# A fused attention and gated-MLP kernel: from the second batch on, product tiles of two banks, and three PSUM banks that gates and side work share in turn

## The chip, the cores and the metric

One core of one Trainium2 chip runs the kernel. The metric is device time in microseconds (us), the median of several runs. A difference of 0.3% (about 2.1 us) is about what a measurement of this kernel can tell from no change.

## What is computed

`x` has 4 batches of 12416 tokens with 128 channels; 32 inducing vectors attend to the tokens of a batch, and then the tokens attend to the 32 results. What comes out goes through a gated MLP with 1536 hidden columns.

```
def mab(q, kv):
    s = scale * (q @ kv.transpose(0, 2, 1))
    s = s - s.max(-1, keepdims=True)
    a = np.exp(s)
    a /= a.sum(-1, keepdims=True) + 1e-09
    return a @ kv
h = mab(I, x)                  # stage 1: 32 results for each batch
attn = mab(x, h)               # stage 2: each token attends to them
gate = 1.0 / (1.0 + np.exp(-(attn @ w_gate)))
val = attn @ w_val
out = (gate * val) @ w_out
```

## The kernel before

**The MLP is the main stream.** The tokens are cut into 97 blocks of 512 (24 in each batch, and one last block of the 4 x 128 tokens left over). The 1536 hidden columns are 12 tiles of 128. The product of h with the weights (`hwt`) is formed once per batch, so that gates and values come from the 32 attention weights of a token (`a2r`) directly: one matmul with 32 rows gives one tile of 128 hidden columns by 512 tokens, which is one PSUM bank. For each tile there are four pieces of work:

- TensorE fills the gate (`g_ps`) and the value (`v_ps`), L1022 in `hidden_mm`.
- ScalarE takes the tanh of half the gate into `t` (L1053; L1045 for a gate tile that stands alone).
- VectorE makes `u = (t + 1) * v` with one SCALAR_TENSOR_TENSOR (L1071, in `product`).
- TensorE multiplies `u` with the output weights and adds up in `acc_ps` (L1106, in `project`, four matmuls for a tile). After 12 tiles ScalarE copies the block out of PSUM (`o`, L1124) and SyncE sends it off.

**Steps.** A step is one value tile, one `u`, and so one VectorE instruction. Until step 608 (`T0`) steps are narrow: a tile of two banks (1024 wide) and a tile of one bank (512 wide) alternate, gates as well as values, so that a block has 8 steps. The eight PSUM banks are then `g2` and `v2` with two banks each, and `g1`, `v1`, `acc` and `m` with one. From `T0` on, in the last 21 blocks, steps are wide: a block has 6 steps of 1024; values alternate between `v2` and `vw` (two banks each), gates are single tiles in `gw0`, `gw1` and `gw2`, and `acc` keeps its bank. The bank `m` is gone by then.

**Side work.** While the MLP of one batch runs, stage 1 of the next batch and stage 2 of the groups to come are worked off beside it: a group is 16 times 128 tokens, four blocks. All of this passes through the bank `m`: scores of stage 2 (`s_ps`, L602, copied out by ScalarE at L636), scores of stage 1 (L236, with a maximum on VectorE, L248, and an exponential, L261, or a plain copy, L358), sums (`hp_ps`, L296, copied at L311 and L421), and small ones for the batch's end (L483, L561, L575). Other parts of it use no PSUM: the exponentials L662 and L407, a maximum on VectorE from SBUF (L389), and the work of GpSimd. The places are numbers: `at(slot, make, late)` puts a piece beside slot `slot`, which is two narrow steps, and `beside` calls it there. A block is four slots. Each engine works its instructions off in the order in which they are written (`manual_schedule`), and waits in place for what an instruction needs.

**Order in a step.** `product(t)` writes the two value matmuls, the gate fills of a later step and the `u`; then come tanh, `project` for the step before, and the side work. In the wide part a step `t` fills and takes the tanh of the single gates 2k+3 and 2k+4 (k is `t - T0`), while its own `u` uses gates 2k and 2k+1. A value tile can be filled once the `u` two steps back is done.

Of the kernel before, what the change touches and what calls it, by code (L numbers as in the profile page):

```python
# [16 lines left out]
P = 128  # L18
# [8 lines left out]
def kernel(  # L27
# [37 lines left out]
    class Banks:  # L65
        pools = {}

# [143 lines left out]
    plan = {}  # L211

    def at(slot, make, late=False):
        plan.setdefault((slot, late), []).append(make)
# [90 lines left out]
    def s1_sum_keep(b, s, hp):  # L305
        ng, w, R = s1_dims(s)
        width = C + 1 if b else C
        summed[b] += 1
        if b == 0 and at_col[s] >= EARLY:
            return hp[:, 0:C]  # L310
        nc.scalar.copy(out=hsts[b % 2][0:R, s1_place(b, s), 0:width], in_=hp[0:R, 0:width])  # L311

    def plan_stage1(b, s, score, total):
        st = {}
        full = groups[s][1] == GC

        def begin():
            st["s1"] = s1_score(b, s, "m")

        def weigh():  # L320
            st["a1T"] = s1_exp(b, s, st["s1"])

        def turn():
            if full:
                st["a1"] = s1_turn_dma(b, s, st["a1T"])
            else:
                st["a1"] = s1_turn_copy(s, s1_turn_pe(b, s, st["a1T"]))

        at(score, begin)
        soon = full  # L330
        at(score + (0 if soon else 1), weigh, late=full)
        at(score + (1 if soon else 2), turn)
        first, second, keep = total

        def part(k0, k1):
            if k0 == 0:
                st["hp"] = ps.tile([P, C + 1], F32, tag="m", name="hp_ps")
            s1_sum_pe(b, s, st["a1"], st["hp"], k0, k1)

        at(first, lambda: part(0, 2))  # L340
        at(second, lambda: part(2, 4))
        at(keep, lambda: s1_sum_keep(b, s, st["hp"]))


    def plan_shared(b, o, takes, tops, least, weighs, sums, holds, one, with_one):
# [11 lines left out]
        def keep(i):  # L357
            nc.scalar.copy(out=place(i), in_=st["s1"][:])  # L358

        def score_one():  # L360
            s1 = s1_score_pe(b, NG, "m")
            st["one"] = s1p.tile([P, 512], F16, tag="a1T", name="one").bitcast(F32)[0:m, 0:P]
            nc.scalar.copy(out=st["one"], in_=s1[0:m, 0:P])
# [55 lines left out]
        def hold(k):  # L419
            summed[b] += 1  # L420
            nc.scalar.copy(out=hst[:, no + k, :], in_=st["hp"][:])  # L421

        for i in range(len(SHARED[b])):
            at(o + takes[i], lambda i=i: score(i))
            at(o + takes[i], lambda i=i: keep(i), late=True)
            at(o + weighs[i], lambda i=i: weigh(i), late=True)
# [4 lines left out]
        at(o + one[1], weigh_one)  # L431
# [6 lines left out]
        for k, slot in enumerate(holds):  # L438
            at(o + slot, lambda k=k: hold(k))
# [68 lines left out]
    def plan_combine(b, lead, weights, joined, taken, fill):  # L508
# [42 lines left out]
        def weight():  # L551
            l_ps = ps.tile([P, 1], F32, tag="m", name="l_ps")
            nc.tensor.matmul(
                l_ps[:],
# [4 lines left out]
            )  # L559
            lx, near, off = (bp.tile([P, 1], F32, tag=f"l{k}", name=f"l{k}") for k in range(3))  # L560
            nc.scalar.copy(out=lx[:], in_=l_ps[:])  # L561
# [11 lines left out]
        def h_keep():  # L573
            hT16[b] = bp.tile([P, m], F16, tag="hT", name="hT")
            nc.scalar.copy(out=hT16[b][:], in_=st["h_ps"][:])  # L575

# [3 lines left out]
        def keep(hf):  # L580
            if hf == 0:
                st["hwt"] = bp.tile([P, NI, P], F16, tag="hw", bufs=B, name="hwt")
            hw_take(st["hwt"], hf, st["hw_ps"])
            if hf == 1:
# [3 lines left out]
        at(weights, weigh)  # L588
        at(joined, join)
        at(joined + 7, weight)  # L590
        at(taken, h_sum)
        at(taken, h_keep)
        for hf, (first, second) in enumerate(fill):
            at(first, lambda hf=hf: part(hf))
            at(second, lambda hf=hf: keep(hf), late=True)
# [115 lines left out]
    def plan_stage2(b, c, score, take, weigh, far=None, soon=False, lag=None, low=None):  # L711
# [30 lines left out]
        def keep():  # L742
            if far is None:
                room()
            s2_take(st["sc"], 0, GC, st["s2"])

# [17 lines left out]

        if far is not None:
            at(far, one)
            at(far + 1, lambda: s2_take(st["sc"], GC, NLO, st["s2"]))
        at(score, lambda: half(0, False))
        at(score + 1, lambda: half(GC // 2, not soon))
# [6 lines left out]
        at(weigh, exp, late=True)  # L776
# [258 lines left out]
    def ring_t(i, n):  # L1035
        c = i % 24 * BC
        return xn[B - 2][:, c : c + n * BC, :].rearrange("p (j a) c -> p j (a c)", a=BC)

    def single_fill(i):
        if i < len(singles):  # L1040
            hidden_mm(singles[i], "g")

    def single_gate(i):
        if i < len(singles):
            nc.scalar.activation(out=ring_t(i, 1), in_=singles[i]["g"][:], func=AF.Tanh, scale=0.5)  # L1045

    def gate(t):
        if t < T0 + 2:
            st = gates[t]
            st["t"] = ring_t(2 * (t - T0), st["cnt"]) if t >= T0 else tp.tile([P, st["cnt"], 512], F16, tag=f"t{st['cnt']}", name="t16")  # L1050
# [6 lines left out]
    def product(t):  # L1057
# [6 lines left out]
        else:  # L1064
            single_fill(2 * (t - T0) + 3)
            single_fill(2 * (t - T0) + 4)
            st["t"] = ring_t(2 * (t - T0), 2)
# [171 lines left out]
    assert not plan  # L1239
# [31 lines left out]
```

## Time and profile before

| | |
|---|---|
| median of 3 runs | 713.9 us (713.79 to 715.37) |
| span of the profiled execution | 712.4 us |
| VectorE (DVE) busy | 694.2 us, 97% |
| ScalarE (ACT) busy | 678.6 us, 95% |
| TensorE (PE) busy, matmuls | 649.5 us, 91% |
| GpSimd (POOL) busy | 449.2 us, 63% |
| first `u` starts | 30.4 us |
| step 192 (second batch) starts | about 201 us |
| step 608 (`T0`) starts | 564.7 us |

The profiled execution's own time is not listed beside its profile; its span from the first to the last instruction is 1.5 us under the median of the runs. An instruction's duration in these views runs from its start until its result is out, and on ScalarE and VectorE the next one can start before that: the distance from one start to the next is what an instruction costs its engine, and it is shorter than its duration. "Busy" is the time in which at least one instruction is under way.

### The profile page before, as it was taken

Reading aid. Unit: us, or ns where it says so; the run is one execution under the profiler, and the core shown is the slowest. Engines: PE = TensorE matmul, PEld = TensorE weight load, DVE = VectorE, ACT = ScalarE, POOL = GpSimd, SP = SyncE. Lnnn points to the kernel's source line nnn. Section 1 sums busy time; section 2 is a strip of 40 time slices with the busy share of each in tenths; the row PEclk is TensorE's granted clock in tenths of the full one; section 3 lists DMA queues with packets and bytes.
Section 4 is the critical chain, followed back from the end, with each engine's and each line's share of the span. In section 5 each row is a group of like instructions: output and inputs, shape, how many; then the busy total and the mean of one; then the engine's idle time right before and its main releaser. Section 6 shows DMA issues by size and latency. Waiting matters only on the chain.

```text
span 712.4 us, 21620 instructions
## 1 busy us (share of the span) xinstructions
PE 649.5 (91%) x8475; PEld 394.2 (55%) x8475; DVE 694.2 (97%) x806; ACT 678.6 (95%) x1103; POOL 449.2 (63%) x785
## 2 busy tenths in 40 slices
PE   7999899998999999999998989999899999899996
PEld 4555455555555555655555655555555555555555
DVE  4799999999999999999999999999999999999997
ACT  4799999999999999999999999999999999999996
POOL 4568865877558978668657887587748356372300
PEclk9999999999999999999999999999999999999999
DMA  8979964263693174155485142221222131221201
GB/s 171 176 136 174 149 129 103 76 120 81 118 159 81 57 126 103 56 120 114 92 149 112 53 76 67 55 76 38 70 76 61 46 60 60 61 61 46 71 37 46
DMA packets 117110, 65.23 MB, mean 92 GB/s; under 512 B 100208, under 2 KB 101392, under 8 KB 117008
## 3 DMA queue, kind: packets, MB, share of 16 engines
q1 hardware_dynamic: 112320, 49.83, 31.4%
q0 software_dynamic: 4416, 13.90, 11.1%
q8 instruction: 66, 1.08, 0.6%
q14 instruction: 36, 0.29, 0.1%
q10 hardware_dynamic: 272, 0.13, 0.1%
HBM read 27.80 MB, written 25.43 MB: 75 GB/s over the span
## 4 chain that ended last, share of the span: by engine, by line
DVE 38%; PE 30%; issue 15%; ACT 14%; DMA 2%; DVEq 1%; POOL 0%; ACTq 0%; POOLq 0%
DVE u L1071 36%; PE acc_ps L1106 14%; PE v_ps L1022 11%; ACT t L1053 11%; PE g_ps L1022 2%; DMA xn<-in_x_dram 2%; ACT o L1124 2%; ACT xn L1045 1%; PE hp_ps L296 1%; DVE nm L248 1%; DVEq L1071 0%; POOL xn L95 0%; ACT a1T L261 0%; ACT e L662 0%; ACT hwt L483 0%
## 5 line engine op out<-in xcount | busy, mean ns | idle before, releaser
L1071 DVE SCALAR_TENSOR_TENSOR u<-t,v_ps 128x512 f16<-128x512 f16 x609 | 528.8, 947 | 1.0 <-ACT t L1053 0.5
L1053 ACT ACTIVATE t<-g_ps 128x512 f16<-128x512 f32 x609 | 464.5, 821 | 11.0 <-ACT t L1053 4.3
L1106 PE MATMUL acc_ps<-wo,u 128*128 128x128 f16 x4656 | 334.5, 220 | 3.2 <-ACT o L1124 0.8
L1106 PEld LDWEIGHTS <-u 128*128 128x128 f16 x4656 | 262.7, 98 | 112.9 <-issue 109.4
L1022 PE MATMUL v_ps<-a2r,hwt 32*128 32x512 f16 (+1 forms) x1188 | 278.6, 372 | 47.1 <-DVE u L1071 43.5
L1022 PE MATMUL g_ps<-a2r,hwt 32*128 32x512 f16 (+1 forms) x1188 | 293.6, 376 | 0.5 <-DVE u L1071 0.2
L1022 PEld LDWEIGHTS <-hwt 32*128 32x128 f16 x2424 | 92.0, 91 | 156.7 <-issue 104.3
L1071 DVE SCALAR_TENSOR_TENSOR u<-xn,v_ps 128x1024 f16<-128x1024 f16 (+1 forms) x127 | 142.9, 1206 | 0.3 <-PE g_ps L1022 0.3
L1045 ACT ACTIVATE xn<-g_ps 128x512 f16<-128x512 f32 x249 | 129.0, 606 | 1.9 <-PE g_ps L1022 0.6
L692 POOL TENSOR_TENSOR a2n<-e,rs 128x2048 f16<-128x2048 f16 (+3 forms) x25 | 86.8, 3475 | 5.0 <-DVE rs L681 2.1
L670 POOL TENSOR_TENSOR sum<-e 128x256 f32<-128x256 f16 (+1 forms) x23 | 15.4, 672 | 117.0 <-ACT e L662 117.0
L453 POOL TENSOR_TENSOR near<-sme,minus 128x16 f32<-128x16 f32 (+1 forms) x22 | 65.2, 2964 | 1.6
L1124 ACT ACTIVATE o<-acc_ps 128x512 f32<-128x512 f32 x96 | 58.0, 604 | 0.0
L647 POOL TENSOR_SCALAR rise<-rise 128x256 f32<-128x256 f32 (+6 forms) x110 | 30.3, 275 | 9.6
L650 POOL TENSOR_TENSOR top<-top,rise 128x128 f32<-128x128 f32 (+3 forms) x88 | 28.5, 323 | 7.3
L670 POOL TENSOR_TENSOR sum<-sum 128x128 f32<-128x128 f32 (+3 forms) x92 | 28.4, 309 | 7.2
L646 POOL TENSOR_TENSOR rise<-top 128x128 f32<-128x128 f32 (+3 forms) x88 | 27.3, 311 | 6.9
L646 POOL TENSOR_TENSOR rise<-sc 128x256 f32<-128x256 f32 (+1 forms) x18 | 13.3, 736 | 21.2 <-ACT sc L636 21.1
L653 POOL TENSOR_TENSOR sc<-sc,top 128x512 f32<-128x512 f32 (+1 forms) x18 | 19.5, 1086 | 1.4
L602 PEld LDWEIGHTS <-xT 128*128 128x128 f16 x388 | 13.1, 96 | 11.7 <-issue 11.3
L95 POOL DMA_DIRECT2D xn<-in_x_dram x25 | 15.0, 607 | 6.5 <-DMA xn<-in_x_dram 5.6
L602 PE MATMUL s_ps<-hT,xT 128*128 128x32 f16 x388 | 18.1, 178 | 0.1
(161 smaller groups left out, 321.7 us busy)
## 6 DMA issues: line engine op xcount, KB each, us to landing
out_dram<-o SPq DMA_DIRECT2D x96, 256.0 KB, 2.1
xn<-in_x_dram POOLq DMA_DIRECT2D x19, 512.0 KB, 7.2
xn<-in_x_dram POOLq DMA_DIRECT2D x4, 544.0 KB, 6.0
a2r<-a2n SPq DMA_TRANSPOSE x29, 4.4
xT<-xn SPq DMA_TRANSPOSE x27, 4.4
xn<-in_x_dram POOLq DMA_DIRECT2D x1, 384.0 KB, 14.9
wg<-in_moe_w_gate_dram POOLq DMA_DIRECT2D x1, 384.0 KB, 16.4
wv<-in_moe_w_val_dram POOLq DMA_DIRECT2D x1, 384.0 KB, 16.4
```

What stands on the lines that cost most here:

```text
L453: nc.gpsimd.tensor_tensor(out=near, in0=x, in1=minus, op=ALU.pow)
L602: nc.tensor.matmul(s2[:, j, :], xT[b][:, c + j, :], hT16[b][:], start=(j == 0), stop=whole and j == j1 - 1, skip_group_check=True,)
L646: nc.gpsimd.tensor_tensor(out=r, in0=far, in1=near, op=ALU.subtract)
L647: nc.gpsimd.tensor_scalar(out=r, in0=r, scalar1=BIG, scalar2=0.0, op0=ALU.min, op1=ALU.max)
L670: nc.gpsimd.tensor_tensor(out=d[:, 0:n, :], in0=src[:, :, 0:w], in1=src[:, :, w : 2 * w], op=ALU.add)
L692: eng.tensor_tensor(out=a2n[:, 0:n, :, :], in0=e.unsqueeze(2).to_broadcast((P, n, 4, m)), in1=rs.unsqueeze(2).unsqueeze(3).to_broadcast((P ...
L1022: st[what + "end"] = nc.tensor.matmul(pt[:, k, col : col + nb * P], hw[b][r : r + 32, j // 2, :], a2r[r : r + 32, o : o + nb, :].rearrange ...
L1045: nc.scalar.activation(out=ring_t(i, 1), in_=singles[i]["g"][:], func=AF.Tanh, scale=0.5)
L1053: st["tanh"] = nc.scalar.activation(out=st["t"][:, :, c:e], in_=st["g"][:, :, c:e], func=AF.Tanh, scale=0.5)
L1071: u = nc.vector.scalar_tensor_tensor(out=st["u"][:, :, c:e], in0=st["t"][:, :, c:e], scalar=1.0, in1=st["v"][:, :, c:e], op0=ALU.add, op1= ...
L1106: nc.tensor.matmul(acc[0][:, i, :], st["u"][:, n, ts(i, P)], wo16[:, NI * (e % 2) + e // 2, :], start=(e == 0 and i == 0), stop=(e == NJ - 1),
L1124: nc.scalar.mul(out=o32[:], in_=acc[0][:], mul=0.5)
```

## The change

Three things change.

**T0 moves.** It was step 608, in the last batch; it is now 192, the first step of the second batch (`T0 = 2 * S0`, with `S0` = 96 slots). The steps from there on are all wide, 73 blocks in place of 21; 52 blocks change their form. The kernel has 630 steps in place of 734. The narrow steps have an added wait of `u` for the gate fill two steps on (the lines with `add_manual_dep`); it goes with them, as it holds for `t < T0` alone.

**One ring for gates and side work.** The wide part has no bank `m`. `gw0`, `gw1` and `gw2` stand in a queue `ring`: a gate fill takes the bank at its head, and the tanh puts it back at the end. Side work takes a bank in the same way (`held`), and `ps.done()`, behind the copy or exponential that empties it, puts it back. One piece of side work at most holds a bank.

**Side work gets places in wide steps.** Slots from `S0` on are turned into steps: `at` multiplies by 1.5, and a piece is put either between the two projections of a step or, with `end=True`, behind the second tanh. A score and the copy that empties its bank now stand in one step; before, they were one or two slots apart, with the two halves of a stage-2 score in slots of their own. Scores of stage 1 hold their bank over two steps, as do sums that join two parts. The tanh results go to two-tile buffers `pair` in the pool `tp` instead of into the space of an old `x`.

The core of the diff:

```diff
         def tile(self, shape, dtype, tag, name):
+            if tag == "m" and self.ring is not None:
+                assert self.held is None and self.ring, name
+                tag = self.held = self.ring.popleft()
             return self.pools[tag].tile(shape, dtype, tag=tag, name=name)
+
+        def done(self):
+            if self.held is not None:
+                self.ring.append(self.held)
+                self.held = None
...
-    def at(slot, make, late=False):
-        plan.setdefault((slot, late), []).append(make)
+    SLOTS = NCH // BC
+    S0 = SLOTS * 4
+    T0 = 2 * S0
+
+    def at(slot, make, late=False, end=False):
+        if slot >= S0:
+            key = (T0 + int((slot + late / 2 - S0) * 1.5 + 0.01), end)
+        else:
+            key = (slot, late)
+        plan.setdefault(key, []).append(make)
...
         def weigh():
             st["a1T"] = s1_exp(b, s, st["s1"])
+            ps.done()
...
-        at(score + (0 if soon else 1), weigh, late=full)
-        at(score + (1 if soon else 2), turn)
+        if score >= S0:
+            at(score + 2 / 3, weigh, end=True)
+            at(score + 2, turn)
+        else:
+            at(score + (0 if soon else 1), weigh, late=full)
+            at(score + (1 if soon else 2), turn)
...
         for i in range(len(SHARED[b])):
+            wide = o + takes[i] >= S0
             at(o + takes[i], lambda i=i: score(i))
-            at(o + takes[i], lambda i=i: keep(i), late=True)
+            at(o + takes[i], lambda i=i: keep(i), late=not wide, end=True)
...
+            if o >= S0:
+                first = o + sums[i // per * per + per - 1] - 2 / 3 * (per - 1 - i % per)
+                at(first, lambda i=i: part(i, 0, 2))
+                at(first, lambda i=i: part(i, 2, 4))
+                continue
...
         at(score, lambda: half(0, False))
-        at(score + 1, lambda: half(GC // 2, not soon))
+        at(score + (0 if wide else 1), lambda: half(GC // 2, not soon))
...
-            at(take, keep, late=True)
+            at(score if wide else take, keep, late=not wide, end=True)
...
-    T0 = first_step[(B - 1, 0)] + 2 * 16
-    assert gates[T0]["j0"] == 0
+    assert gates[T0]["j0"] == 0 and first_step[(1, 0)] == T0
...
-        singles += [dict(block=i, j0=j, cnt=1, bank=f"gw{j % 3}") for j in range(NJ)]
+        singles += [dict(block=i, j0=j, cnt=1) for j in range(NJ)]
...
     def single_fill(i):
         if i < len(singles):
+            singles[i]["bank"] = ps.ring.popleft()
             hidden_mm(singles[i], "g")
 
     def single_gate(i):
         if i < len(singles):
-            nc.scalar.activation(out=ring_t(i, 1), in_=singles[i]["g"][:], func=AF.Tanh, scale=0.5)
+            nc.scalar.activation(
+                out=pair(i // 2)[:, i % 2 : i % 2 + 1, :],
+                in_=singles[i]["g"][:],
+                func=AF.Tanh,
+                scale=0.5,
+            )
+            ps.ring.append(singles[i]["bank"])
...
     ps.open(ctx, "psw", "vw", "gw0", "gw1", "gw2")
+    ps.ring = deque(["gw0", "gw1", "gw2"])
     for t in range(T0, NST):
         product(t)
-        six, part = divmod(t - T0, 3)
         single_gate(2 * (t - T0) + 3)
         for i in range(2):
             if not project(t - 1, t, 1) and waiting(t - 1) >= 2:
                 project(t - 1, t, 1)
             if i == 0:
-                for slot, late in ([(0, False), (0, True)], [(1, False)], [(1, True)])[part]:
-                    beside(T0 // 2 + 2 * six + slot, late)
+                beside(t, False)
         single_gate(2 * (t - T0) + 4)
+        beside(t, True)
```

How the instructions move on ScalarE, in the second batch's MLP where stage 1 of the third batch runs beside it (`t` is a tanh, `e` the exponential of a stage-2 group, `hst` a copy of a sum, `o` a finished block, `sc` the copy of a stage-2 score). In the kernel before:

```order
L662 ACTIVATE e<-sc 128x512
L1053 ACTIVATE t_5185<-g_ps 128x1024
L311 COPY hst_143<-hp_ps 128x129
L1053 ACTIVATE t_5222<-g_ps 128x512
L1053 ACTIVATE t_5244<-g_ps 128x1024
L1053 ACTIVATE t_5261<-g_ps 128x512
L1124 ACTIVATE o_5275<-acc_ps 128x512
L1053 ACTIVATE t_5286<-g_ps 128x1024
L1053 ACTIVATE t_5310<-g_ps 128x512
L1053 ACTIVATE t_5333<-g_ps 128x1024
L1053 ACTIVATE t_5341<-g_ps 128x512
L636 COPY sc<-s_ps 128x512
```

The same stretch in the changed kernel, with line numbers of its own (`x2` is two like instructions in a row):

```order
L711 ACTIVATE e<-sc 128x512
L329 COPY hst_143<-hp_ps 128x129
L1103 ACTIVATE t_5179<-g_ps 128x512
L1103 ACTIVATE t_5214<-g_ps 128x512 x2
L1103 ACTIVATE t_5234<-g_ps 128x512 x2
L1103 ACTIVATE t_5271<-g_ps 128x512
L685 COPY sc<-s_ps 128x512
L1103 ACTIVATE t_5271<-g_ps 128x512
L1191 ACTIVATE o_5301<-acc_ps 128x512
L1103 ACTIVATE t_5304<-g_ps 128x512 x2
```

Each tanh is now 512 wide, and the pieces of side work stand closer together: between `e` and `sc` there were 8 tanh with 12 tiles in all; now there are 6 tiles.

On TensorE, at the first stage-2 score of the second batch's MLP (`v_ps` and `g_ps` are the value and gate fills, numbered by tile, `s2_ps` the score, `acc_ps` the projection). Before:

```order
L1022 MATMUL v_ps_4564<-a2r_4078,hwt_3665 128x512
L1022 LDWEIGHTS hwt_3665
L1022 MATMUL g_ps_4567<-a2r_4078,hwt_3665 128x512
L1022 LDWEIGHTS hwt_3665
L1022 MATMUL g_ps_4567<-a2r_4078,hwt_3665 128x512
L602 LDWEIGHTS xT_1_880
L602 MATMUL s2_ps_4574<-hT_3382,xT_1_880 128x32
```

And in the changed kernel:

```order
L1076 MATMUL v_ps_4564<-a2r_4078,hwt_3665 128x512
L1076 LDWEIGHTS hwt_3665
L1076 MATMUL g_ps_4567<-a2r_4078,hwt_3665 128x512
L1076 LDWEIGHTS hwt_3665
L1076 MATMUL g_ps_4569<-a2r_4078,hwt_3665 128x512
L1173 LDWEIGHTS u16_4531
L1173 MATMUL acc_ps_4485<-wo16_112,u16_4531 128x128
```

Where the two matmuls of one gate tile (`g_ps_4567`) stood side by side, there are now two tiles with a bank each, `g_ps_4567` and `g_ps_4569`, and the projection stands behind both of them; the score, all 16 matmuls of it, follows behind four matmuls of the projection, where before it stood in two halves of 8 at places of their own.

More of the change, by code (lines that the diff above doesn't have):

```diff
@@ L2 @@
+from collections import deque
 from contextlib import ExitStack
@@ L66 @@
         pools = {}
+        ring = None
+        held = None
         def open(self, stack, name, *tags):
@@ L338, in part @@
             s1_sum_pe(b, s, st["a1"], st["hp"], k0, k1)
+        if first >= S0:
+            second = keep = first
         at(first, lambda: part(0, 2))
         at(second, lambda: part(2, 4))
-        at(keep, lambda: s1_sum_keep(b, s, st["hp"]))
+        at(keep, lambda: s1_sum_keep(b, s, st["hp"]), end=True)
     def plan_shared(b, o, takes, tops, least, weighs, sums, holds, one, with_one):
@@ L438, in plan_shared @@
         for k, slot in enumerate(holds):
-            at(o + slot, lambda k=k: hold(k))
+            if o >= S0:
+                slot = sums[k * per + per - 1]
+            at(o + slot, lambda k=k: hold(k), end=True)
     hT16 = {}
@@ L587, in plan_combine @@
         at(lead, least)
-        at(weights, weigh)
+        at(weights, weigh, end=True)
         at(joined, join)
         at(joined + 7, weight)
+        at(joined + 7, invert, end=True)
         at(taken, h_sum)
-        at(taken, h_keep)
+        at(taken, h_keep, end=True)
         for hf, (first, second) in enumerate(fill):
             at(first, lambda hf=hf: part(hf))
-            at(second, lambda hf=hf: keep(hf), late=True)
+            if first >= S0:
+                at(first, lambda hf=hf: keep(hf), end=True)
+            else:
+                at(second, lambda hf=hf: keep(hf), late=True)
     a2 = {}
```

48 lines of the change are left out of this document (34 added, 14 removed).

## The prediction

> **What bounds the kernel now.** I read the page first, for what is full; then the groups of instructions kept apart by shape; then the timeline of single engines, for the distance from one instruction to the next.
>
> ```profile
> PE 649.5 (91%) x8475; PEld 394.2 (55%) x8475; DVE 694.2 (97%) x806; ACT 678.6 (95%) x1103; POOL 449.2 (63%) x785
> ...
> DVE  4799999999999999999999999999999999999997
> ...
> DVE 38%; PE 30%; issue 15%; ACT 14%; DMA 2%; DVEq 1%; POOL 0%; ACTq 0%; POOLq 0%
> ```
>
> VectorE is at 9 tenths or more from the third slice to the last but one, and it leads the chain. ScalarE's 95% looks as full, so the next question is whether both bound it. The stretch that changes form, steps 192 to 607, against the stretch that is wide already:
>
> ```profile
> 200.95:564.73 363.78, 336.18 (x4459) 205.00 (x4458) 363.69 (x424) 357.04 (x542) 259.54 (x448) 1.00 0.38 85
> 566.22:703.00 136.78, 125.40 (x1499) 75.73 (x1499) 136.78 (x121) 135.41 (x267) 54.87 (x86) 1.00 0.20 56
> ```
>
> The third pair is DVE: 363.69 of 363.78 us, and all of 136.78. It waits for nobody in either form. That ACT (fourth) waits can't be seen here, since an ACTIVATE counts as busy until its result is out. The timeline shows it:
>
> ```profile
> 600.80 2.06 ACT L1045 ACTIVATE xn<-g_ps 128x512 f16<-128x512 f32 x4
> ...
> 602.23 0.63 ACT L1045 ACTIVATE xn<-g_ps 128x512 f16<-128x512 f32 x1
> ```
>
> The second row, asked for by itself, is the last of the four tanh in the first: from 600.80 to 602.23 are three turns of 0.477 us. That is ACT's turn when its input is there; the group has a longer mean, and two in five have a wait of 17 ns in front of them (the EVENT_SEMAPHORE row):
>
> ```profile
> L1045 ACTq EVENT_SEMAPHORE  x106: 17/17/17, 565.3 to 705.1; - x106
> ...
> L1045 ACT ACTIVATE xn<-g_ps 128x512 f16<-128x512 f32 x249 | 129.0, 606 | 1.9 <-PE g_ps L1022 0.6
> ```
>
> 129.0 / 249 = 0.518 us for each: 0.04 of that is waiting inside "busy". So DVE alone is the bound, and ACT has some room.
>
> **The change part by part.** *DVE's turns.*
>
> ```profile
> 245.79 136.37 DVE L1071 SCALAR_TENSOR_TENSOR u<-t,v_ps 128x1024 f16<-128x1024 f16 x157
> ...
> 566.22 137.07 DVE L1071 SCALAR_TENSOR_TENSOR u<-xn,v_ps 128x1024 f16<-128x1024 f16 x121 [0.27 <-PE g_ps L1022]
> ```
>
> The first row is the narrow form, alternately 1024 and 512 (a merged row is named by its first). Less the last one's 1.22 us, 156 turns take 135.15, so a pair takes 1.733 and a block of four pairs 6.931. The second row is wide: 120 turns in 135.85, 1.132 each, and a block of six 6.793. Two instructions fewer per block save 0.138 us; 52 blocks change form, so the gain is 7.2 us if DVE stays the bound. The measured stretch gives the upper end: 363.78 less its six maxima is 361.0, 6.942 a block, so 52 x (6.942 - 6.793) = 7.8 us, as some small stalls are in it. The maxima stay; their turns:
>
> ```profile
> 214.22 0.68 DVE L248 TENSOR_REDUCE nm<-s_ps 128x1 f32<-128x512 f32 x1
> 214.82 7.08 DVE L1071 SCALAR_TENSOR_TENSOR u<-t,v_ps 128x512 f16<-128x512 f16 x8
> ...
> 243.27 0.28 DVE L389 TENSOR_REDUCE nm<-xT 128x1 f32<-128x128 f32 x1
> 243.47 138.70 DVE L1071 SCALAR_TENSOR_TENSOR u<-t,v_ps 128x512 f16<-128x512 f16 x160
> ```
>
> 0.60 and 0.20 us; a batch has two and one, 1.4 us.
>
> *ACT's turns.* A narrow gate pair costs ACT two turns for three tiles, the wide form three. The side work keeps its cost, and these are its large groups in the stretch that changes:
>
> ```profile
> L636 ACT COPY sc<-s_ps 128x512 f32<-128x512 f32 x12 | 7.1, 592 | 0.0
> L662 ACT ACTIVATE e<-sc 128x512 f16<-128x512 f32 x10 | 6.4, 639 | 0.0
> L407 ACT ACTIVATE a1T<-xT 128x512 f16<-128x512 f32 x8 | 5.1, 636 | 0.0
> L358 ACT COPY xT<-s_ps 128x512 f32<-128x512 f32 x7 | 4.1, 592 | 0.0
> L261 ACT ACTIVATE a1T<-s_ps,nm 128x512 f16<-128x512 f32 x4 | 2.7, 687 | 0.5
> L483 ACT CAST hwt<-hw_ps 128x384 f16<-128x384 f32 x4 | 1.9, 485 | 0.0
> L311 ACT COPY hst<-hp_ps 128x129 f32<-128x129 f32 x4 | 1.2, 296 | 0.0
> ...
> 300.94 0.60 ACT L1124 ACTIVATE o<-acc_ps 128x512 f32<-128x512 f32 x1
> 301.42 3.10 ACT L1053 ACTIVATE t<-g_ps 128x1024 f16<-128x1024 f32 x4
> 304.40 0.59 ACT L636 COPY sc<-s_ps 128x512 f32<-128x512 f32 x1
> 304.87 3.11 ACT L1053 ACTIVATE t<-g_ps 128x1024 f16<-128x1024 f32 x4
> ```
>
> An `o` of 0.60 has its follower 0.48 later, an `sc` of 0.59 after 0.47: a turn is the mean less 0.12. By that the shown groups are 22.7 us of turns, and with the smaller ones I estimate 28 us in 52 blocks, 13 us in the 24 of a batch. A whole wide batch then asks of ACT 288 x 0.477 = 137.4 for the tanh, some 2.1 for semaphore waits of 17 ns in two of five, 24 x 0.477 = 11.4 for the `o`, and 13.0: 163.9 us (0.484 a turn with the waits, over 312 turns). DVE's own is 144 x 1.132 + 1.4 = 164.4. This is the price of the change: in the second and third batch ACT has 0.5 us to spare in 164, and lumps of side work are never made good quickly. In the stretch that the order rows show, from `e` to the second tile behind `o`, five steps hold ten tanh, `e` 0.52, `hst` 0.18, `sc` 0.47 and `o` 0.48: 6.4 us against DVE's 5 x 1.132 = 5.7.
>
> *The lead that covers a lump.* A step of the wide form as it runs now, first TensorE, then ACT's two tanh and the `u`:
>
> ```profile
> 603.22 0.62 PE L1106 MATMUL acc_ps<-wo,u 128*128 128x128 f16 x8
> 603.78 0.39 PE L1022 MATMUL v_ps<-a2r,hwt 32*128 32x512 f16 x2
> ...
> 604.92 0.39 PE L1022 MATMUL g_ps<-a2r,hwt 32*128 32x512 f16 x2
> 605.25 0.62 PE L1106 MATMUL acc_ps<-wo,u 128*128 128x128 f16 x8
> 606.05 0.39 PE L1022 MATMUL v_ps<-a2r,hwt 32*128 32x512 f16 x2 [0.18 <-DVE u L1071]
> ...
> 605.38 0.60 ACT L1045 ACTIVATE xn<-g_ps 128x512 f16<-128x512 f32 x1
> 605.87 0.59 ACT L1045 ACTIVATE xn<-g_ps 128x512 f16<-128x512 f32 x1
> 605.91 1.21 DVE L1071 SCALAR_TENSOR_TENSOR u<-xn,v_ps 128x1024 f16<-128x1024 f16 x1
> ```
>
> With three free banks the second gate fill of a step waits for the first tanh of the step before; where side work holds a bank, it waits for the second, done at 606.46, and not at 605.98. TensorE works in order, so projection and next value fill queue behind that fill. From 606.51: the projection 0.33 later (604.92 to 605.25), the next value fill 0.56 after that (603.22 to 603.78), done in 0.39, at 607.79. Its `u` is due at 605.91 + 2 x 1.132 = 608.17. So ACT may be late by about 0.4 us in a step whose side work holds a bank, and by 0.9 in others, before DVE waits. Now a running sum over the steps in the order of the changed kernel: add ACT's turns, take off 1.132 (and DVE's maxima), never below zero; what stands above the lead is a wait of DVE and is taken off. It gives 1.3 us in each of the second and third batch and 0.1 in the last, whose side work is thin. With 0.9 throughout it is 0.7 a batch; with 0.4 throughout 4.5, 4.9 and 2.5, 12.0 in all. I take 1.5 for each of the two, 3.0 in all: nearer the low end, since about 26 of 144 steps hold a bank, and a little over the sum for the side matmuls in the same TensorE queue.
>
> *At nothing.* TensorE's matmuls are the same in number; a step takes it 0.33 + 0.56 = 0.9 of 1.132 us, and the 0.18 us that it waits for `u` is what is left to see of that. Whole scores in one step put 16 matmuls where 8 stood; if that cover is gone, a value fill is late by some tenths, which the 0.3 us over the sum are for. GpSimd and SyncE keep their work and, but for a few neighbours that change places, its order; GpSimd is busy 259.54 of 363.78 us, so a batch that is 2% shorter leaves it room. The switch of banks costs 0.27 us of waiting (the row at 566.22) at either place of `T0`. The dropped wait of `u` for a gate fill has no waiting of DVE to give back.
>
> *The sum.* -7.2 + 3.0 = -4.2 us. The profiled span is 712.4, 1.5 under the median of the runs; I carry the difference over: 713.9 - 4.2 = 709.7 us.
>
> **The rivals.** *The lead suffices* (the ring is never short): waits of 0 to 1.4 us, a gain of 5.8 to 7.8, 706.1 to 708.1. For it: DVE shows no wait now in wide steps with the same lead. Against: none of those has side work in PSUM.
>
> *The waits eat the gain:* with a lead of 0.5 to 0.7 throughout, waits of 5.1 to 9.3 us, a time within 2.1 us of now.
>
> *ACT becomes the bound, slower than before.* If a tanh of 512 cannot follow the one before sooner than the group's 0.518, a dense batch asks 312 x 0.518 + 13.0 = 174.6 us of ACT, 10.2 over DVE's 164.4; for two batches 20.4, less 7.2: 713.9 + 13.2 = 727.1. It decides from 0.485 us a turn on, where ACT's sum passes DVE's, and slower begins at about 0.50. Against it is the row of four at 0.477; for it, that 0.518 is the mean. The Trainium skill speaks for this one: ScalarE: Activation LUTs, section What ACT_TABLE_LOAD costs, gives an ACTIVATE 186 ns + 0.833 ns an element, with neighbours overlapping by 93 ns. By that a turn of 512 would be an estimated 0.52 us, each split tanh would pay the fixed 0.09 once more, and the time would be the rival's; the row of four, at 0.477, does not agree.
>
> *The ring itself, slower:* side pieces that stand in neighbouring steps leave TensorE waiting at the second fill each time. With a lead of 0.2 throughout, the running sum is 25.5 us, and the time 732; slower begins where the lead is under about 0.5 throughout. Against it: the working above, 0.9 in most steps.
>
> **How the numbers follow.** Forecast, a gain of 2.1 to 5.8 us: 0.46. The lead suffices: 0.16. The gain eaten, within 2.1 us: 0.20. Slower: 0.18, half of it for ACT's turn and half for the ring. So faster by over 0.3% 0.62, within 0.20, slower 0.18; 0.3% is 2.1 us, about what a measurement of this kernel can tell from no change. The range goes from 706.1, less 0.4 for the spread of runs, 705.7, to 716.0, where waits of 9.3 us would be: it leaves out slower, 0.18, and little else.
>
> **What would show it.** Right: in the wide part of the second and third batch the distance between `u` is 1.132 us in most steps, with single waits of 0.1 to 0.5 us near lumps of side work, some 3 us in all; a block takes 6.86 us there, and the last batch 6.8. ACT's idle time hardly shows. Wrong: distances of `u` over 1.17 on average (ACT or the ring bounds), a wait of TensorE for ACT tanh in most steps, or GpSimd late, with ACT waiting for it in front of `e`.

## The result, and the profile after

The changed kernel takes 726.4 us (726.28 to 726.46, 4 runs) against 713.9: 1.017 times the time before, interval 1.016 to 1.019. The forecast was 709.7 us, faster; the kernel is slower.

The three batches after the first, in the profile after (columns: the window and its length, the busy time and the number of instructions of PE, PEld, DVE, ACT and POOL, then the granted clock, DMA share and GB/s; in the last of the three only the first 24 steps change form):

```profile
200.79:374.96 174.17, 163.47 (x2056) 88.21 (x2057) 167.69 (x148) 169.84 (x347) 123.70 (x215) 1.00 0.49 100
374.96:549.18 174.22, 163.28 (x2070) 88.64 (x2071) 167.81 (x148) 169.98 (x349) 119.66 (x208) 1.00 0.29 68
549.18:718.60 169.42, 156.35 (x1914) 93.83 (x1913) 169.01 (x149) 167.16 (x330) 71.20 (x116) 1.00 0.20 56
```

The second and third batch, 192 narrow steps each, in the profile before:

```profile
200.95:368.87 167.92, 154.90 (x2056) 94.18 (x2056) 167.92 (x197) 164.81 (x252) 123.77 (x214) 1.00 0.49 101
368.87:536.80 167.93, 155.38 (x2069) 94.82 (x2068) 167.84 (x196) 164.69 (x251) 119.95 (x207) 1.00 0.31 73
```

Here, in two batches of 144 wide steps, are the 12 us: 6.3 us each. VectorE has fewer instructions (148 for 197), and 6.5 us in each batch in which it does nothing; it did nothing for 0.1 us or less before. The clock is full in all of them. VectorE's own turns are 164.4 us, as forecast, so in 174.2 it waits for 9.8 us, the part that the view counts as busy included, and about 1 us in the last batch: 20.6 us of waits, of which 3.0 were forecast. TensorE now leads the chain that ended last, with 51% in place of 30%, and VectorE has 16% in place of 38%:

```profile
PE 51%; ACT 21%; DVE 16%; issue 9%; DMA 2%; POOL 0%; DVEq 0%; POOLq 0%; ACTq 0%
```

One such wait from close by, the longest of the second batch: the timeline of TensorE, then of ScalarE, then of VectorE, after.

```profile
216.64 0.39 PE L1076 MATMUL v_ps<-a2r,hwt 32*128 32x512 f16 x2
216.65 0.57 PE L1076 MATMUL g_ps<-a2r,hwt 32*128 32x512 f16 x2
217.15 0.40 PE L1173 MATMUL acc_ps<-wo,u 128*128 128x128 f16 x4
217.48 0.23 PE L254 MATMUL s_ps<-xT,indT 128*32 128x128 f16 x1
217.64 0.40 PE L1173 MATMUL acc_ps<-wo,u 128*128 128x128 f16 x4
217.97 0.39 PE L1076 MATMUL v_ps<-a2r,hwt 32*128 32x512 f16 x2
217.97 0.38 PE L1076 MATMUL g_ps<-a2r,hwt 32*128 32x512 f16 x1
219.21 0.37 PE L1076 MATMUL g_ps<-a2r,hwt 32*128 32x512 f16 x1 [0.85 <-ACT t L1103]
219.51 0.62 PE L1173 MATMUL acc_ps<-wo,u 128*128 128x128 f16 x8
220.07 0.39 PE L1076 MATMUL v_ps<-a2r,hwt 32*128 32x512 f16 x2
```

```profile
218.07 0.60 ACT L1191 ACTIVATE o<-acc_ps 128x512 f32<-128x512 f32 x1 [0.30 <-PE acc_ps L1173]
218.57 0.59 ACT L1103 ACTIVATE t<-g_ps 128x512 f16<-128x512 f32 x1
219.04 0.24 ACT L392 COPY one<-s_ps 32x128 f32<-32x128 f32 x1
```

```profile
214.99 4.69 DVE L1138 SCALAR_TENSOR_TENSOR u<-t,v_ps 128x1024 f16<-128x1024 f16 x4
220.55 2.54 DVE L1138 SCALAR_TENSOR_TENSOR u<-t,v_ps 128x1024 f16<-128x1024 f16 x2 [0.87 <-PE g_ps L1076]
```

The side score (L254) holds a bank and puts off the block's last projection, so ScalarE's `o` waits for it (0.30), and the second tanh stands behind `o`. It ends at 219.16. The next step's second gate fill needs that tanh's bank: it starts at 219.21, 1.24 us behind its neighbour, and TensorE lies idle for 0.85 of it, with projection and next value fill behind. That fill starts at 220.07, and the `u` for it at 220.55, 0.87 late. In the two dense batches, the second and third, TensorE's four fills of a step start 0.23 us apart from first to last (32 us in 144 steps); in the wide part of the kernel before it was 0.13. This spread alone is no measure of the loss: in e9 below, where VectorE waits for half as long, it is 37 us a batch. Nearly every wait of VectorE ends 0.10 us after a value fill does; in most of them the gates had been ready for 0.3 to 1 us.

### The profile page after: what moved, and what is told of

Its sections match the earlier page's. It is cut to its first block, busy times and chain, and to the rows that moved or that the text cites. A ratio compares the mean times of both kernels' runs of the same rounds, so it can differ in the third digit from the quotient of the medians.

```text
span 724.6 us, 21472 instructions
## 1 busy us (share of the span) xinstructions
PE 666.1 (92%) x8475; PEld 380.9 (53%) x8475; DVE 693.6 (96%) x702; ACT 689.4 (95%) x1311; POOL 447.8 (62%) x785
## 4 chain that ended last, share of the span: by engine, by line
PE 51%; ACT 21%; DVE 16%; issue 9%; DMA 2%; POOL 0%; DVEq 0%; POOLq 0%; ACTq 0%
PE acc_ps L1173 26%; DVE u L1138 15%; PE v_ps L1076 14%; ACT t L1103 13%; PE g_ps L1076 8%; ACT o L1191 5%; ACT t L1120 3%; DMA xn<-in_x_dram 2%; PE hp_ps L314 1%; PE s_ps L651 1%; PE s_ps L254 1%; DVE nm L266 0%; POOL xn L106 0%; DVEq L1138 0%; PE aT_ps L292 0%
## 5 line engine op out<-in xcount | busy, mean ns | idle before, releaser
L1138 DVE SCALAR_TENSOR_TENSOR u<-t,v_ps 128x1024 f16<-128x1024 f16 (+2 forms) x632 | 670.9, 1128 | 14.2 <-PE g_ps L1076 6.8
L1103 ACT ACTIVATE t<-g_ps 128x512 f16<-128x512 f32 x873 | 451.4, 612 | 6.8 <-PE g_ps L1076 5.3
L1173 PEld LDWEIGHTS <-u 128*128 128x128 f16 x4656 | 267.1, 98 | 212.6 <-issue 208.1
L1173 PE MATMUL acc_ps<-wo,u 128*128 128x128 f16 x4656 | 360.2, 220 | 15.2 <-ACT o L1191 12.4
L1076 PE MATMUL g_ps<-a2r,hwt 32*128 32x512 f16 (+1 forms) x1188 | 306.6, 373 | 10.1 <-ACT t L1103 5.2
L1076 PE MATMUL v_ps<-a2r,hwt 32*128 32x512 f16 (+1 forms) x1188 | 240.5, 375 | 22.6 <-DVE u L1138 18.3
L1120 ACT ACTIVATE t<-g_ps 128x512 f16<-128x512 f32 x195 | 148.5, 820 | 4.8 <-ACT t L1120 2.1
L1076 PEld LDWEIGHTS <-hwt 32*128 32x128 f16 x2424 | 78.0, 91 | 98.9 <-issue 38.2
L405 POOL TENSOR_TENSOR xT<-xT 128x512 f32<-128x512 f32 (+2 forms) x13 | 12.4, 954 | 14.6 <-ACT xT L384 9.4
L651 PE MATMUL s_ps<-hT,xT 128*128 128x32 f16 x388 | 15.3, 177 | 0.1
## 6 DMA issues: line engine op xcount, KB each, us to landing
wg<-in_moe_w_gate_dram POOLq DMA_DIRECT2D x1, 384.0 KB, 16.3
```

The lines of the kernel that those rows point to most:

```text
L651: nc.tensor.matmul(s2[:, j, :], xT[b][:, c + j, :], hT16[b][:], start=(j == 0), stop=whole and j == j1 - 1, skip_group_check=True,)
L1076: st[what + "end"] = nc.tensor.matmul(pt[:, k, col : col + nb * P], hw[b][r : r + 32, j // 2, :], a2r[r : r + 32, o : o + nb, :].rearrange ...
L1103: nc.scalar.activation(out=pair(i // 2)[:, i % 2 : i % 2 + 1, :], in_=singles[i]["g"][:], func=AF.Tanh, scale=0.5,)
L1120: st["tanh"] = nc.scalar.activation(out=st["t"][:, :, c:e], in_=st["g"][:, :, c:e], func=AF.Tanh, scale=0.5)
L1138: u = nc.vector.scalar_tensor_tensor(out=st["u"][:, :, c:e], in0=st["t"][:, :, c:e], scalar=1.0, in1=st["v"][:, :, c:e], op0=ALU.add, op1= ...
L1173: nc.tensor.matmul(acc[0][:, i, :], st["u"][:, n, ts(i, P)], wo16[:, NI * (e % 2) + e // 2, :], start=(e == 0 and i == 0), stop=(e == NJ - 1),
```

## The experiments

The times are medians; the kernel before ran on the same chip each time (medians of 713.9 to 714.1 us, and beside the last one 714.0 to 716.5). Differences are against the 726.4 us of the changed kernel, and under about 2 us they tell little. The theories, as they were named on the way: **H**, the ring: where side work holds a bank, the second fill waits; in **L** that is one place of a loop of TensorE and ScalarE, in which the projection behind `o` is another; **R** is what is left of both, the held banks. **B**: whole scores and sums in one step are too much for TensorE at a time. **A**: ScalarE has more work than time; in **S** it has just as much as time, so that its waits are lost. "Dense" batches are the second and third.

**Two banks for gates always (e1).**

```diff
-                assert self.held is None and self.ring, name
-                tag = self.held = self.ring.popleft()
+                tag = "gw2"
...
-    ps.ring = deque(["gw0", "gw1", "gw2"])
+    ps.ring = deque(["gw0", "gw1"])
```

> Edit: side work has one bank of its own (gw2) and the gates take turns in two; nothing else moves. Theory H (the ring: when side work holds a bank, the second gate fill of a step must wait for the tanh that has just begun, and TensorE, which works in order, holds projection and next value fill behind it): now every step has two banks for gates, so steps without side work stall as well, and the time is over 735. Theory B (whole scores and sums in one step are too much for TensorE at once) and theory A (ScalarE has more work than time): order and amount are the same, 724 to 728.

823.2 us, 97 more than the changed kernel, over 438 steps. VectorE and ScalarE (from the groups by shape):

```profile
L1137 DVE SCALAR_TENSOR_TENSOR u<-t,v_ps 128x1024 f16<-128x1024 f16 x532 | 632.1, 1217 | 93.3 <-ACT t L1102 44.6 <-PE g_ps L1075 29.1 <-ACT sc L684 1.9
L1102 ACT ACTIVATE t<-g_ps 128x512 f16<-128x512 f32 x873 | 476.1, 596 | 62.1 <-PE g_ps L1075 61.8
```

ScalarE waits for gate fills and the fills for ScalarE. Two banks don't carry the stream, as H said. A fill of 0.38 and a tanh of 0.60 with the gaps between them make an estimated 1.1 us for a bank, and each of the two has to turn once in a step of 1.13, so next to nothing is left. Where side work is thin, the trace has this row once a block:

```profile
665.43 7.26 DVE L1137 SCALAR_TENSOR_TENSOR u<-t,v_ps 128x1024 f16<-128x1024 f16 x6 [0.81 <-ACT t L1102]
```

That is 1.21 us a step, (7.26 - 1.22) / 5, and 0.81 more once a block, behind `o`.

**The second tanh ahead of o (e2).**

```diff
         single_gate(2 * (t - T0) + 3)
+        single_gate(2 * (t - T0) + 4)
         for i in range(2):
...
-        single_gate(2 * (t - T0) + 4)
         beside(t, True)
```

> Edit: the second tanh of a step is written ahead of the two projections, so that the copy o of a finished block stands behind it on ScalarE and not in front. Theory H, with the wait of o for its projection as what makes the second tanh late: the waits in the two steps behind each block end go, 712 to 720. Theory B: 724 to 728. Theory A: the idle time of ScalarE in front of o, about 0.3 us a block, goes, but its work stays, 721 to 726.

727.2 us, no gain. The fills' spread falls from 32 to 24 us a batch, and the same time returns elsewhere. The group of projections, after and in this kernel:

```profile
L1173 PE MATMUL acc_ps<-wo,u 128*128 128x128 f16 x4656 | 360.2, 220 | 15.2 <-ACT o L1191 12.4 <-DVE u L1138 0.4
```

```profile
L1173 PE MATMUL acc_ps<-wo,u 128*128 128x128 f16 x4656 | 360.2, 220 | 41.3 <-ACT o L1191 40.4 <-DVE u L1138 0.4
```

The next block's projection waits for `o` for 40 us in place of 12. The order of the two only chooses which wait it is.

**The second fill behind the first projection (e3), and both (e4).**

```diff
             single_fill(2 * (t - T0) + 3)
-            single_fill(2 * (t - T0) + 4)
...
             if i == 0:
+                single_fill(2 * (t - T0) + 4)
                 beside(t, False)
```

> Edit: the second gate fill of a step is written behind the first projection, in place of ahead of it. Theory H: half of the projection no longer queues behind the fill that waits, 0.2 to 0.3 us of lead more in each step whose side work holds a bank, 712 to 720. Theory B: no change, 724 to 728. Theory A: 724 to 728.

> Edit: both of the two: second gate fill behind the first projection, and the second tanh ahead of side work and of o. Theory H: 706 to 714, the waits nearly gone. Theories A and B: over 720.

826.3 and 836.0 us. These say nothing for or against the theories, since the edit has a price of its own. TensorE in e3, where side work is thin:

```profile
662.01 0.39 PE L1076 MATMUL v_ps<-a2r,hwt 32*128 32x512 f16 x2
662.01 0.38 PE L1076 MATMUL g_ps<-a2r,hwt 32*128 32x512 f16 x1
662.33 0.40 PE L1172 MATMUL acc_ps<-wo,u 128*128 128x128 f16 x4
662.66 0.39 PE L1076 MATMUL g_ps<-a2r,hwt 32*128 32x512 f16 x1
662.98 0.40 PE L1172 MATMUL acc_ps<-wo,u 128*128 128x128 f16 x4
663.31 0.39 PE L1076 MATMUL v_ps<-a2r,hwt 32*128 32x512 f16 x2
```

A fill that stands alone takes TensorE 0.32 us until the next projection starts (662.66 to 662.98), as much as three fills in groups of 32 rows take together (662.01 to 662.33), and a step is 1.30 us of TensorE without a pause.

**Side work two steps later (e5).**

```diff
-            key = (T0 + int((slot + late / 2 - S0) * 1.5 + 0.01), end)
+            key = (T0 + 2 + int((slot + late / 2 - S0) * 1.5 + 0.01), end)
```

> Edit: all side work of the wide part two steps later, so that its pieces stand at other places of the six-step block; nothing else. Theory L (a loop: TensorE, in order, waits for ScalarE at the second gate fill and at the projection behind o, and each wait makes ScalarE's next tanh late; the changed kernel waits 0.22 us a step at the second fill where the wide part of before waits 0.12): the place against the block's end, where o stands, matters, so the time moves by 2 to 6 us either way. Theory B (the side matmuls, whole scores and sums in one step, fill TensorE): the same bursts, 725.5 to 727.5. Theory A (ScalarE has more work than time): 725.5 to 727.5.

726.9 us: the place against `o` doesn't matter in sum. L's forecast, 2 to 6 us either way, fails here.

**What frees the bank ahead of the second tanh (e6).** `beside(t, True)` and `single_gate(2 * (t - T0) + 4)` change places.

> Edit: the copy or exponential that frees the side work's bank, and what else is put at a step's end, stands ahead of the second tanh and not behind it. So the second fill of the next step takes the bank of the side work, which is free one tanh sooner. Theory L: 715 to 722. Theory B: 725 to 728. Theory A: 725 to 728.

733.0 us, 6.6 worse. The bank comes free sooner, but the copy stands first in ScalarE's queue, waits there for the score (11 copies `sc` wait for 2.4 us in all in this trace, one at 212.06 for 0.19), and puts off the tanh. No theory had the time longer than 728.

**Scores in halves again (e7).**

```diff
-        at(score + (0 if wide else 1), lambda: half(GC // 2, not soon))
+        at(score + (2 / 3 if wide else 1), lambda: half(GC // 2, not soon))
...
-            at(score if wide else take, keep, late=not wide, end=True)
+            at(score + 2 / 3 if wide else take, keep, late=not wide, end=True)
```

> Edit: a stage-2 score is again two halves of 8 matmuls in neighbouring steps, and its copy stands in the second; its bank is held for two steps. Theory B: the burst is halved, 718 to 723. Theory L: the bank is held for twice as long, 727 to 735. Theory A: 725 to 728.

742.6 us, 16 worse and more than any theory said, with half the burst and the bank held for two steps. (Its two runs had granted clocks of 0.989 and 0.993, so a part of the 16 may be the clock's.) For B this is no proof by itself, since the longer hold covers what a smaller burst may give; e16 puts a number on the burst. If all of it is the hold, a step more costs at most about 0.9 us a score (16.3 us over 19 scores).

**Side matmuls behind both projections (e8), and e2 with it (e12).** `beside(t, False)` stands behind the loop of projections.

> Edit: the side matmuls of a step stand behind both projections and not between them, so that they no longer put off a finished block's o. Theory L: where side work stands in the step of o, that wait goes, 720 to 725, as few pieces stand there. Theory B: the same matmuls before the same next value fill, 725 to 728. Theory A: 725 to 728.

> Edit: second tanh ahead of the projections, and side matmuls behind them (the orders of two kernels before, together). Theory L: o no longer waits for side matmuls and the second tanh no longer for o: 718 to 723. Theory R: what counts are the held banks, as many as before: 722 to 727.

724.3 and 727.1 us: 2 us for the first, in L's range and about the least that a measurement here can tell, and nothing left of it in the second, where L forecast 718 to 723.

**No bank held (e9).** In the wide part, a tile for side work is SBUF, and its matmuls are left out:

```diff
             if tag == "m" and self.ring is not None:
-                assert self.held is None and self.ring, name
-                tag = self.held = self.ring.popleft()
+                n = shape[1] * (shape[2] if len(shape) > 2 else 1)
+                v = wg16[:].bitcast(F32)[:, 0:n]
+                return v.rearrange("p (j k) -> p j k", j=shape[1]) if len(shape) > 2 else v
```

> Leaves out all side matmuls of the wide part; ScalarE's and VectorE's side instructions stay, but read a tile in SBUF (weights, as numbers) where they read PSUM. So no side work holds a bank, and the gates have three throughout. Theory R (a bank held by side work makes TensorE, in order, wait at the second gate fill; what the loop of L comes down to): the waits go, and the wide form's gain is left, 705 to 710. Theory A (ScalarE has more work than time: its instructions are all there): 722 or more.

716.5 us: 9.9 of the 20 us go, more than A and less than R said. The dense batches take 169.8 and 169.3 us in place of 174.2. With three banks throughout and no side matmuls, the wide form is still 0.3% slower than the kernel before (1.0031, 1.0017 to 1.0045). There is a second cause.

**The same for stage-2 scores alone (e10).**

> The same for the stage-2 scores alone, 19 of the 56 steps in which side work holds a bank; their matmuls are left out and their copies read SBUF. Theory R: 19 of 56 of the 21 us of waits go, some 7 us, 717 to 721. Theory A: 725 to 728. (Theory B had its burst halved without gain; if it were right all the same, 717 to 721 too, as the matmuls go.)

724.8 us in the median of two runs, 726.0 and 723.5: 1.6 less, not 7. The slower of the two is the profiled one, and it lost time ahead of the change. The narrow part, which this edit doesn't touch, took 203.7 us in place of 200.8, at a clock of 0.97 in its first 50 us, where the changed kernel's was 1.00. The dense batches of the same trace:

```profile
203.67:376.75 173.08, 161.90 (x1959) 86.11 (x1960) 167.06 (x149) 169.28 (x347) 123.67 (x215) 1.00 0.49 101
376.75:549.33 172.58, 161.59 (x1957) 86.07 (x1958) 166.84 (x148) 169.30 (x349) 119.68 (x208) 1.00 0.28 67
```

They are 1.1 and 1.6 us shorter than in the changed kernel, and the other run, at a clock of 1.00, is 2.8 us faster. By count, 19 of 56 banks of the 9.9 us of e9 would be 3.4. So R's 7 was wrong because R put all 21 us on the banks; bank by bank the price is much the same.

**Side exponentials twice (e11).** The two ACTIVATEs of the side work's exponentials (L711 and L437 of the changed kernel) stand in a loop of two, in the wide part.

> Edit: the 24 exponentials of side work in the wide part that read SBUF are done twice, 24 x 0.52 = 12.5 us more for ScalarE; no bank is held for longer. Theory A: the time grows by 10 to 13 us, 736 to 740. Theory R: ScalarE waits some 10 us in each of the two dense batches, and takes part of it there: 727 to 733.

742.9 us, 16.5 more, and more than the 12.5 us of added work that was reckoned with. The second exponential of a pair starts 0.70 us after the first in the trace, not 0.52, and the pair below takes 1.24 us of ScalarE's turns:

```profile
267.24 1.33 ACT L713 ACTIVATE e<-sc 128x512 f16<-128x512 f32 x2
268.48 3.04 ACT L1105 ACTIVATE t<-g_ps 128x512 f16<-128x512 f32 x6
```

24 times 0.70 is 16.8, so the changed kernel takes in nothing of it.

**Side exponentials left out (e13), and no banks either (e14).**

```diff
         def weigh(i):
+            if o + weighs[i] >= S0:
+                st["a1T"] = wv16[:, 0:512]
+                return
...
         def exp():
+            if weigh >= S0:
+                st["e"] = wg16[:, 0 : (GC + NLO) * m].rearrange("p (j k) -> p j k", k=m)
+                return
```

> Leaves out the 24 exponentials of side work in the wide part that read SBUF; what reads their results reads weights instead. Banks, rings and side matmuls are as in the changed kernel. Theory S (in the dense batches ScalarE's turns, 163.5 us, are as long as VectorE's 164.4, so its waits for TensorE, 10.6 us a batch, can't be made up): 5.2 us of turns less in each of two batches and 2.1 in the last, 714 to 718. Theory R (the held banks alone): nearly the same waits, 723 to 726.5.

> Leaves out both: those 24 exponentials, and all side matmuls of the wide part (side instructions read SBUF, no bank is held). Theory S with R beside it: ScalarE has 5 us to spare in a batch and few waits, so the wide form's own gain is left, 706 to 709. If something else bounds the wide form, 712 or more.

721.3 us, 5.1 less, with all banks held: between the ranges of S and R, so neither theory alone is right. And 709.3 us with both left out, 17.1 less. VectorE in the changed kernel, in e13 and in e14 (the last columns are idle time in front of it):

```profile
L1138 DVE SCALAR_TENSOR_TENSOR u<-t,v_ps 128x1024 f16<-128x1024 f16 x532 | 617.6, 1213 | 13.4 <-PE g_ps L1076 6.5 <-ACT t L1103 3.6 <-issue 0.2
```

```profile
L1144 DVE SCALAR_TENSOR_TENSOR u<-t,v_ps 128x1024 f16<-128x1024 f16 x532 | 616.1, 1216 | 10.3 <-PE g_ps L1082 6.0 <-ACT t L1109 1.8 <-issue 0.6
```

```profile
L1145 DVE SCALAR_TENSOR_TENSOR u<-t,v_ps 128x1024 f16<-128x1024 f16 x532 | 612.4, 1216 | 1.7 <-ACT t L1110 0.3 <-PE g_ps L1083 0.3 <-issue 0.2
```

e14 is 0.9935 of the time before (0.9917 to 0.9953): the wide form's own gain is there, 4.7 of the forecast 7.2 us, once side work takes nothing from the ring and these exponentials nothing from ScalarE. (The kernel before without the same side work was not run; VectorE hardly waits in it.)

**The same exponentials twice in the kernel before (e15).**

> The kernel before, with the same 24 exponentials done twice that cost the changed kernel 16.5 us. Theory S: in the narrow form ScalarE has some 10 us to spare in a batch, so the 7 us a batch are taken in: 713.5 to 716. If an exponential costs its time wherever it stands (by a wait of GpSimd for it, say), 722 or more.

729.9 us, 15.8 more (1.0212, 1.0140 to 1.0284), where S forecast 713.5 to 716. This goes against S as it was put: the narrow form has some 10 us of ScalarE's time to spare in a batch and can't take in 7 either. Its timeline shows why, VectorE around three double exponentials:

```profile
259.70 7.01 DVE L1073 SCALAR_TENSOR_TENSOR u<-t,v_ps 128x1024 f16<-128x1024 f16 x8 [0.53 <-PE v_ps L1024]
267.23 13.93 DVE L1073 SCALAR_TENSOR_TENSOR u<-t,v_ps 128x1024 f16<-128x1024 f16 x16 [0.52 <-PE g_ps L1024]
281.73 7.00 DVE L1073 SCALAR_TENSOR_TENSOR u<-t,v_ps 128x1024 f16<-128x1024 f16 x8 [0.57 <-PE v_ps L1024]
```

ScalarE (same kernel) just ahead of the first two:

```profile
257.02 1.29 ACT L408 ACTIVATE a1T<-xT 128x512 f16<-128x512 f32 x2
...
264.55 1.29 ACT L664 ACTIVATE e<-sc 128x512 f16<-128x512 f32 x2
```

Each pair is 1.2 us of ScalarE's turns and costs VectorE one wait of 0.5 to 0.6 us, and then nothing for 6 to 14 us. So the narrow form's cover is, by estimate, a lead of about 0.65 us (1.20 less 0.55), which a single exponential of 0.52 fits in and which is full again when the next one comes. Spare time over a batch is not what counts here; what counts is a lump against the lead, and how soon the lead returns.

**One matmul for each score or sum, banks held as before (e16).**

```diff
+        if ps.ring is not None:
+            nc.tensor.matmul(s1[:], wo16[:, 0, :], wg16[:, 0:512], start=True, stop=True)
+            return s1
```

(and likewise in the scores of stage 2 and the sums)

> Leaves out most side matmuls of the wide part: each score or sum is one matmul of 512 (or 129) columns on weights, which writes the same bank; banks are held from step to step as in the changed kernel, and ScalarE's work is the same. If of the 9.9 us that went with banks and matmuls the held banks are the cause: 724 to 727. If the matmuls' time on TensorE is: 716 to 719.

724.4 us: 2 of the 9.9 us of e9 are the matmuls' time, and the other 8 go with the held banks. The medians come from different chips and leave that uncertain by some 2 us; the traces say the same, as the dense batches take 173.3 and 173.4 us here, against 169.8 and 169.3 in e9. e9 also took away the copies' wait for their scores, which isn't told apart from the banks. With e7 this leaves little of theory B.

## Why the prediction was wrong, point by point

**VectorE's turns: right.** Undisturbed, `u` follows `u` after 1.131 us, and a dense batch's turns are 164.4 us. The gain of 7.2 us was spent on waits. e14, without the side work's claims, shows 4.7 of it.

**ScalarE's turns: right in number.** 312 turns of 0.484 and 13.0 of side work were forecast at 163.9 us a dense batch. Summed up pair by pair in the trace after, with the shortest distance that each kind of pair has anywhere in it, they are 163.5 (162 to 164, by how pairs are sorted into kinds).

**The lead that covers a lump: this is the step that failed.** The running sum of ScalarE's lateness against leads of 0.4 and 0.9 us "gives 1.3 us in each of the second and third batch", taken as 1.5; it was 9.8. What the runs show in its place: about 8 us go with the held banks and 2 with the side matmuls (e9, e16), 5.1 with the side exponentials (e13), and 2.1 more go only when both are left out (e14).

Three things were missing from the sum; that they made it short is argued from the rows, and no run parts them. First, it counted ScalarE's turns but none of its own waits for TensorE. A size for them stood in the prediction: 0.518 less 0.484 is 0.034 us a turn, over 312 turns 10.6 us a batch. It was read as room. With turns of 163.5 in 164.4 us there is no room, and a wait of ScalarE that isn't made good elsewhere is lost. That 163.5 + 10.6 = 174.1 comes so near to the batch's 174.2 is luck, though, for the waits are no constant: in e9, with the same turns, the dense batches take 169.8 and 169.3, so ScalarE waits for about 6 us; in e13, with ten exponentials fewer in each, they take 172.2 and 171.6, so it waits for 12 or more. Second, the sum started each step with a TensorE that was on time. But its spare time is 0.2 us a step, and a held bank takes 0.5 from the lead at the second fill (0.9 to 0.4 in the prediction's own working; 0.85 of waiting at 219.21 above), so its delay can go on into the next steps. Third, 0.9 us was taken as the lead of steps without a held bank, whatever had stood before them. And "nearer the low end" was a choice for the wrong row: the measured 20.6 lies between the rows for a lead of 0.4 throughout, 12.0 in all, and of 0.2 throughout, 25.5.

**The rivals.** "ACT becomes the bound, slower than before", at 727.1 us, had the right figure by luck and a part of the cause: the turns stayed at 0.48, where it needed 0.518, but ScalarE, almost full, takes in nothing of what is added (e11). The estimate of 0.52 us a turn that the prediction worked out from the Trainium skill's page ScalarE: Activation LUTs, section What ACT_TABLE_LOAD costs, would have led to about that figure; the turn of 0.477 doesn't bear it out. "The ring itself, slower" is the other part: of the 20.6 us, e9 takes 9.9 with banks and matmuls, 8 of them with the banks by e16, e13 takes 5.1 with the exponentials, and both together 17.1, 2.1 more than their sum. The lead being enough, and the gain just eaten, were not what happened.

**At nothing.** That whole scores in one step cost little holds: all side matmuls together are about 2 us (e16). The switch of banks costs 0.26 us of waiting, 0.27 before, and no wait of VectorE for GpSimd shows in the trace after.

**No better kernel.** The wide form lost more than its 0.55 us in each 24 steps of the two dense batches, and in the first 24 of the last batch too (1.0 us); from there on it is the kernel before. No reordering here came nearer to it than 724.3.

**What stays open:** which of the three missing things cost how much, and what VectorE still waits for in e14. Its two dense batches are 166.4 and 165.6 us long there, 3.2 us over the turns of 164.4; that covers the 2.5 us between its gain and the forecast one.

## What to carry to other kernels

When an instruction form that saves time on the bound engine makes another engine's turns as long, that engine's waits count too. Look at the waits inside its busy time in the nearest stretch of the same form before calling it covered; they are a warning and not a figure to add, since they were 6 us a batch in e9 and over 10 in the changed kernel. Side work is covered piece by piece, by the lead at its place and by the time until the lead is back, not by spare time over a batch. A buffer lent from a ring takes from the ring's lead, and on an engine whose instructions are in a fixed order the fill that waits holds up everything behind it.

## What the runs showed of the hardware that was not expected

Fills on 32 rows cost TensorE about 0.3 us before a full-height matmul starts, and here it was the same for one, three or four of them: four fills at 604.92 and the projection at 605.25 in the kernel before; three at 662.01 and the projection at 662.33, one at 662.66 and the projection at 662.98 in e3. Splitting one off cost 100 us over 438 steps (e3). And a bank that is filled in 0.38 us and read in 0.60 by ScalarE takes more than the sum of the two, 0.98, to turn: an estimated 1.1 us with the gaps. Two such banks gave steps of 1.21 us in place of 1.13, and 0.81 us more at each `o` (e1). The same ACTIVATE written twice into the same tile takes 0.66 to 0.73 us for the first of the two, where one followed by a tanh takes 0.52 to 0.56 (e11, e15).
